# Decayed causal attention in front of a mixer MLP: two key blocks per query block, guarded by a test on the chip, and attention spread over the whole program

## The chip, the cores and the metric

The kernel runs on one core of one Trainium2 chip. The time is the device time in microseconds (us) of one execution. Every comparison below was run in rounds on one chip, with the kernel before run in the same rounds. The ratios use fast runs only. Because the program uses one core, a run can be called slow only by being more than 1.5% above the fastest run of the same kernel.

## The reference

Eight batches, eight heads, 576 tokens, head dimension 64. Attention has a causal mask and a bias that decays with the distance in a running sum of `s`. Its output, with the heads side by side (512 channels), goes through a mixer: an MLP over the tokens (576 to 256 to 576) with a residual, then an MLP over the channels (512 to 1536 to 512) with a residual.

```python
scores = scale * np.matmul(q, k.transpose(0, 1, 3, 2))          # scale = 1/8
cum = np.cumsum(np.maximum(s, 0.0), axis=-1)
bias = -(cum[:, :, :, None] - cum[:, :, None, :])
scores = np.where(causal, -1000000000.0, scores + np.minimum(bias, 0.0))
scores = scores - np.max(scores, axis=-1, keepdims=True)
attn = np.exp(scores)
attn = attn / (np.sum(attn, axis=-1, keepdims=True) + 1e-09)
x = ...np.matmul(attn, v), heads side by side: (8, 576, 512)
h = np.maximum(x.transpose(0, 2, 1) @ w_tok1, 0.0) @ w_tok2
u = x + h.transpose(0, 2, 1)
out = u + np.maximum(u @ w_ch1, 0.0) @ w_ch2
# inputs: s is drawn as randn * 0.5; q, k and v as randn * 0.1
```

The bias of key j seen from query i is `cum[j] - cum[i]`. The part `-cum[i]` is the same for all keys of a row and cancels in the softmax, so the kernel works with unnormalised weights `exp(score) * exp(cum[j] - cum[end]/2)`: the second factor is multiplied into v once.

## The kernel before

Work is recorded as operations in a plan: each has the tiles that it reads and writes, the engines that may do it with an assumed cost, and a priority. A list scheduler on the host picks, for each engine, the ready operation of lowest priority, and so fixes the order of every engine's instructions before the launch. The engines then run that order in sequence. An operation late in its engine's order waits there even if its data is ready early.

Attention goes by pairs of heads (32 pairs). Per pair, q and k are transposed, and scores are computed transposed (keys on partitions) in seven pieces that cover the causal half of 576 x 576:

```python
PIECES = [[(0, 0, 256)], [(0, 256, 512)], [(0, 512, 576), (1, 384, 576)], [(1, 128, 384)],
          [(2, 256, 512)], [(2, 512, 576), (3, 384, 576)], [(4, 512, 576)]]   # (key block, first query, last query)
...
for pc, piece in enumerate(PIECES):
    ...
        for (jc, a, e, c0) in cols:                                            # L473, PE
            nc.tensor.matmul(out=o[:, :, c0 : c0 + e - a], lhsT=kT.t[:, jc * 128 : jc * 128 + 128],
                             rhs=qT.t[:, :, a:e], start=True, stop=True)
    P.op({"PE": (occ, occ + 0.3, mm)}, ..., prio=(1, pi, 1))
    for (jc, a, e, c0) in cols:
            nc.scalar.activation(out=E.t[:, :, d0 : d0 + e - a], in_=i[:, :, c0 : c0 + e - a],
                                 func=AF.Exp, scale=0.125)                     # L481, ACT
            ...
            nc.vector.tensor_tensor(out=E.t[:, :, d0 : d0 + n], ...            # L489, DVE: causal mask of the
                in1=keep[:, 0:n]..., op=ALU.mult)                              # diagonal block, both inputs in SBUF
...
for ic in range(NJ):                                                           # L510, PE: 15 per head
    for jc in range(ic + 1):
        nc.tensor.matmul(out=o[:, ic, 0 : D + 1], lhsT=E.t[:, hh, d0 : d0 + 128],
                         rhs=vp.t[:, jc, h + hh, 0 : D + 1], start=(jc == 0), stop=(jc == ic))
```

The priorities decide how attention and the MLP are mixed. In the kernel before, the token MLP of batch `unit` has `(0, unit, ...)`, the attention pair `pi` has `(1, pi, ...)` and the channel MLP has `(2, unit, ...)`. So a pair always goes ahead of channel work, and channel work fills what is left; attention is over at about 235 us and the rest is MLP alone.

Weights arrive as fp32, are staged in the buffers that later hold the hidden layer of the channel MLP, and are cast to bf16 on whichever engine the plan chose. PE is TensorE, ACT is ScalarE, DVE is VectorE, POOL is GpSimd. "c1" and "c2" below are the first and second channel layer.

The softmax here doesn't subtract the row's maximum and nothing guards it: scores larger than these inputs give would overflow.

## Time and profile before

| | value |
|---|---|
| time | 373.82 us median of 3 runs (373.78 to 378.82) |
| span of the profiled run | 373.2 us |
| PE busy | 91% |
| start of the first c2 matmul | 84.88 us |
| end of the last add | 369.17 us, 4.0 us before the end of the span |

From the page of the kernel before, the span, the busy times of the engines, and the busy tenths of PE, DVE, ACT and DMA in 40 slices of the span:

```profile
span 373.2 us, 7668 instructions
PE 340.0 (91%) x2949; PEld 198.0 (53%) x2949; DVE 207.2 (56%) x498; ACT 228.3 (61%) x504; POOL 93.5 (25%) x129
...
PE   1875987989999989998999999999999999999994
DVE  7897577597778878667886667513302302302021
ACT  4795794877669768777878686750460660450810
DMA  9999999999996382616122010002102002102012
```

PE is nearly full from the tenth slice on (9 is 90% or more; two slices before the last show 8). DVE and ACT are well loaded up to slice 26; after that DVE is down to 0 to 3 tenths and ACT works in bursts: attention has ended. The DMA engines are full for the first 12 slices, 112 us.

A busy PE is not a PE at its limit, because matmuls overlap. The Trainium skill says so too ("Trainium Kernel Development and Optimization", Performance Expectations: matmul busy time is a bad measure because matmuls are pipelined). So I count PE **issue**: the time from start to start in back-to-back streams, 216 ns for 512 columns, 30 ns for an AV matmul, about 45 ns for a q/k transpose. The first of these can be read off the last twelve matmuls of c2 in the timeline of the kernel before (start, duration, engine, line, operation, count):

```profile
365.69 2.75 PE L688 MATMUL pmx_118<-wc_68,gb_108 128*128 128x512 bf16 x12
```

The last of the twelve takes 379 ns by itself (the mean of this group on the page), so (2.75 - 0.379) / 11 = 216 ns from start to start. Summed over the instructions, the issue is 318.5 us before: q/k transposes 17.3, scores 43.2, AV 28.8, token layers 34.6, transposes of u 8.1, channel layers 93.3 each (the terms add up to 318.6 because each is rounded). What the span has beyond that, 54.7 us, is time in which PE had nothing to start.

### The profile page before, as it was taken

How to read it: one execution, taken by the hardware profiler on the slowest of the kernel's cores; microseconds unless marked ns; L12 is line 12 of the kernel's file. 1: busy time of each engine (PE TensorE's matmuls, PEld its weight loads, DVE VectorE, ACT ScalarE, POOL GpSimd, SP SyncE). 2: the span in 40 equal slices, each digit the busy share in tenths (PEclk: the TensorE clock that was granted, in tenths of full speed). 3: DMA queues.
4: the chain of work that ended last, by engine and by line, in shares of the span. 5: the costliest groups of instructions: out<-in, count | busy, mean ns of one | idle time of the engine just before them, and what ended most of it. 6: DMA issues, size and time to landing. Idle time of an engine off the chain costs nothing.

```text
span 373.2 us, 7668 instructions
## 1 busy us (share of the span) xinstructions
PE 340.0 (91%) x2949; PEld 198.0 (53%) x2949; DVE 207.2 (56%) x498; ACT 228.3 (61%) x504; POOL 93.5 (25%) x129
## 2 busy tenths in 40 slices
PE   1875987989999989998999999999999999999994
PEld 0543535446657657564555656764444664445741
DVE  7897577597778878667886667513302302302021
ACT  4795794877669768777878686750460660450810
POOL 2427733274443552643342300000000000000000
PEclk9999898999999999999999999999999999999998
DMA  9999999999996382616122010002102002102012
GB/s 183 259 333 231 256 291 210 193 317 241 271 223 154 99 181 70 190 57 198 52 65 64 31 58 29 2 2 92 50 0 84 31 0 86 56 2 88 24 58 85
DMA packets 59173, 45.87 MB, mean 123 GB/s; under 512 B 39296, under 2 KB 52160, under 8 KB 59136
## 3 DMA queue, kind: packets, MB, share of 16 engines
q1 hardware_dynamic: 59136, 45.38, 47.7%
q8 instruction: 23, 0.38, 0.4%
q14 instruction: 14, 0.11, 0.1%
HBM read 35.93 MB, written 9.44 MB: 122 GB/s over the span
## 4 chain that ended last, share of the span: by engine, by line
PE 68%; DVE 13%; DMA 8%; ACT 7%; issue 2%; POOL 1%; SPq 0%; ACTq 0%; DVEq 0%; POOLq 0%
PE pmx_118 L688 9%; PE pmx_120 L688 8%; PE pmx_120 L669 8%; PE pmx_119 L669 7%; PE pmx_118 L669 7%; PE pmx_119 L688 6%; DMA gb_108<-in_moe_w_ch_dram 4%; PE psc_114 L473 3%; PE psc_115 L473 3%; PE psc_113 L473 3%; DMA qkf_73<-in_k_dram 3%; PE pmx_119 L603 2%; PE pav_117 L510 2%; DVE ua_101 L630 2%; PE pav_116 L510 2%
## 5 line engine op out<-in xcount | busy, mean ns | idle before, releaser
L669 PEld LDWEIGHTS <-wc_67 128*128 128x128 bf16 x576 | 55.7, 98 | 37.4 <-issue 1.9
L688 PEld LDWEIGHTS <-gb_108 128*128 128x128 bf16 x240 | 23.1, 98 | 26.3 <-issue 0.4
L688 PEld LDWEIGHTS <-ga_107 128*128 128x128 bf16 x192 | 18.3, 97 | 19.8 <-issue 0.5
L489 DVE TENSOR_TENSOR E_86<-E_86,keep 128x256 bf16<-128x256 bf16 (+1 forms) x55 | 18.6, 355 | 11.3 <-ACT E_86 L481 10.9
L385 POOL TENSOR_TENSOR vp_91<-vf_89,wT 128x512 bf16<-128x512 f32 (+1 forms) x20 | 20.6, 1058 | 14.9 <-PE pav_117 L510 13.1
L489 DVE TENSOR_TENSOR E_87<-E_87,keep 128x256 bf16<-128x256 bf16 (+1 forms) x50 | 18.9, 391 | 9.7 <-ACT E_87 L481 9.2
L489 DVE TENSOR_TENSOR E_85<-E_85,keep 128x256 bf16<-128x256 bf16 (+1 forms) x55 | 22.3, 425 | 3.6 <-ACT E_85 L481 3.3
L669 PE MATMUL pmx_119<-uTb_106,wc_67 128*128 128x320 bf16 x132 | 23.3, 299 | 0.0
L669 PE MATMUL pmx_120<-uTb_106,wc_67 128*128 128x320 bf16 x132 | 23.3, 299 | 0.0
L669 PE MATMUL pmx_118<-uTb_106,wc_67 128*128 128x320 bf16 x120 | 21.2, 299 | 0.0
L688 PE MATMUL pmx_118<-wc_68,ga_107 128*128 128x512 bf16 x84 | 20.6, 379 | 0.0
L676 ACT ACTIVATE ga_107<-pmx_120 128x512 bf16<-128x512 f32 x16 | 9.6, 601 | 17.6 <-PE pmx_120 L669 17.4
L688 PE MATMUL pmx_118<-wc_68,gb_108 128*128 128x512 bf16 x84 | 20.1, 379 | 0.0
L688 PE MATMUL pmx_120<-wc_68,gb_108 128*128 128x512 bf16 x84 | 19.9, 379 | 0.0
L676 ACT ACTIVATE gb_108<-pmx_120 128x320 bf16<-128x320 f32 x26 | 11.4, 437 | 13.9 <-PE pmx_120 L669 11.9
L676 ACT ACTIVATE gb_108<-pmx_119 128x320 bf16<-128x320 f32 x27 | 11.9, 439 | 12.9 <-PE pmx_119 L669 10.7
L669 PE MATMUL pmx_120<-uTa_105,wc_67 128*128 128x512 bf16 x76 | 19.5, 379 | 0.0
L481 ACT ACTIVATE E_85<-psc_115 128x128 bf16<-128x128 f32 (+2 forms) x37 | 15.8, 462 | 3.7 <-PE psc_115 L473 3.7
L481 ACT ACTIVATE E_86<-psc_114 128x512 bf16<-128x512 f32 (+2 forms) x36 | 15.8, 467 | 3.3 <-PE psc_114 L473 2.8
L481 ACT ACTIVATE E_85<-psc_113 128x512 bf16<-128x512 f32 (+2 forms) x31 | 15.3, 511 | 3.4 <-PE psc_113 L473 3.4
L688 PE MATMUL pmx_119<-wc_68,gb_108 128*128 128x512 bf16 x72 | 16.8, 379 | 0.0
L481 ACT ACTIVATE E_86<-psc_115 128x512 bf16<-128x512 f32 (+2 forms) x28 | 14.1, 520 | 3.9 <-PE psc_115 L473 3.9
(289 smaller groups left out, 783.2 us busy)
## 6 DMA issues: line engine op xcount, KB each, us to landing
gb_108<-in_moe_w_ch_dram SPq DMA_DIRECT2D x6, 768.0 KB, 8.8
vf_88<-in_v_dram SPq DMA_DIRECT2D x16, 256.0 KB, 5.3
vf_89<-in_v_dram SPq DMA_DIRECT2D x16, 256.0 KB, 7.9
qkf_69<-in_k_dram SPq DMA_DIRECT2D x11, 288.0 KB, 4.2
qkf_70<-in_q_dram SPq DMA_DIRECT2D x11, 288.0 KB, 4.9
qkf_71<-in_k_dram SPq DMA_DIRECT2D x11, 288.0 KB, 4.8
qkf_72<-in_q_dram SPq DMA_DIRECT2D x11, 288.0 KB, 5.2
qkf_73<-in_k_dram SPq DMA_DIRECT2D x10, 288.0 KB, 5.1
```

What stands on the lines that cost most here:

```text
L385: eng.tensor_tensor(out=vp.t[0:n, c, :, 0:D], in0=vf.t[0:n, c, :, :], in1=wT[0:n, c, b * H : b * H + H].unsqueeze(2).to_broadcast([n, H, D ...
L473: nc.tensor.matmul(out=o[:, :, c0 : c0 + e - a], lhsT=kT.t[:, jc * 128 : jc * 128 + 128], rhs=qT.t[:, :, a:e], start=True, stop=True)
L481: nc.scalar.activation(out=E.t[:, :, d0 : d0 + e - a], in_=i[:, :, c0 : c0 + e - a], func=AF.Exp, scale=0.125)
L489: nc.vector.tensor_tensor(out=E.t[:, :, d0 : d0 + n], in0=E.t[:, :, d0 : d0 + n], in1=keep[:, 0:n].unsqueeze(1).to_broadcast([128, 2, n]), ...
L510: nc.tensor.matmul(out=o[:, ic, 0 : D + 1], lhsT=E.t[:, hh, d0 : d0 + 128], rhs=vp.t[:, jc, h + hh, 0 : D + 1], start=(jc == 0), stop=(jc ...
L603: nc.tensor.matmul(out=pm.t[:, :], lhsT=w1[odd][:, c, t * 128 : t * 128 + 128], rhs=x.t[:, c, :], start=(c == 0), stop=(c == NJ - 1))
L630: nc.vector.tensor_tensor(out=dst.t[lo:hi, di, :], in0=pm.t[lo:hi, :], in1=x.t[lo:hi, c, :], op=ALU.add)
L669: nc.tensor.matmul(out=pm.t[:, 0 : e - a], lhsT=wc1[:, m, cc * 128 : cc * 128 + 128], rhs=uT.t[:, m, a:e], start=(m == 0), stop=(m == NMC ...
L676: lambda cc=cc, pm=pm, a=a, e=e: nc.scalar.activation(out=g.t[:, cc, a:e], in_=pm.t[:, 0 : e - a], func=AF.Relu),
L688: nc.tensor.matmul(out=pm.t[:, :], lhsT=g.t[:, cc, c * 128 : c * 128 + 128], rhs=wc2[:, cc, :], start=(cc == 0), stop=(cc == NCC - 1))
```

## The change

The decay makes far keys vanish. So each 128-query block looks only at its own key block and the one before it. That is safe only if the decay is strong enough over the skipped keys and no score is large, so a test on the chip checks it: a scan of the decay weights, the total decay, and the sums of squares of q and k, each over twelve rows of 64. If any entry fails, a branch at the end recomputes everything for all keys with a slow, plain routine (its body is left out below).

```diff
-    PIECES = [[(0, 0, 256)], [(0, 256, 512)], [(0, 512, 576), (1, 384, 576)], [(1, 128, 384)],
-              [(2, 256, 512)], [(2, 512, 576), (3, 384, 576)], [(4, 512, 576)]]
+    PIECES = [[(0, 0, 256)], [(1, 128, 384)], [(2, 256, 512)], [(3, 384, 576), (4, 512, 576)]]
...
-            for (jc, a, e, c0) in cols:
-                def ex(...):                       # one Exp per entry of the piece: nine per pair
+            def ex(ps=ps, pc=pc):                  # one Exp per piece: four per pair
+                nc.scalar.activation(out=E.t[:, :, EB[pc] : EB[pc] + 256],
+                                     in_=ps.t[:, :].rearrange("p (e n) -> p e n", e=2), func=AF.Exp, scale=0.125)
...
-                    for jc in range(ic + 1):
+                    j_lo = max(ic - 1, 0)
+                    for jc in range(j_lo, ic + 1):  # AV: nine per head instead of fifteen
...
+            P.op(act(768, lambda n=n, col=col: nc.scalar.activation(      # 64 of these on ACT
+                out=junk[:, :], in_=n.t[:, :, :, :].rearrange("p r e d -> p (r e d)"), func=AF.Square,
+                accum_out=sq[:, col : col + 1])), reads=[(n, 0)], writes=[("sq", col)], prio=3)
...
+    P.op(dve(64, lambda: nc.vector.tensor_scalar(
+        out=bad[0:PR, 4:], in0=sq[:, :], scalar1=10.5, scalar2=None, op0=ALU.is_gt)), ...)
+    # bad is summed over partitions by a matmul with ones, then on DVE into one int32 flag
+    need = nc.values_load(flagi[0:1, 0:1], min_val=0, max_val=4096)
+    with tc.If(need > 0, preferred_fallthrough_block=False):
+        general(ctx, tc, q, k, v, out, cum, ident, w1, w2, wc1, wc2)
...
-   pair: prio=(1, pi, i)      tok: prio=(0, unit, i)        c1: prio=(2, unit, 0)                c2: prio=(2, unit, 1)
+   pair: prio=(np_, i)        tok: prio=(rank - TOK, i)     c1: prio=(rank + 2.0 * cc / NCC, 0)  c2: prio=(rank + 2.0 + 2.0 * c / NJ, 1)
+   np_ = (b * H + h) / 2      rank = 4 * (b + 1) + LAG, LAG = TOK = 2.0
```

The last lines gather the changes of priority in one place. There are 4 pairs per batch, so `np_` and `rank` count in the same unit: the channel work of a batch is now spread over four pairs, beginning two pairs after its own last one. The change also stores the last 64 rows of odd batches differently (one copy of `w1` instead of two, no pads in `E`), which I treat as part of the window.

On these inputs the recomputation isn't taken: worked out on the host, the worst decay is 0.49 of its limit, the largest sum of squares 9.13 against 10.5, the largest total decay 132 against 160. So no run here takes the branch, and whether the recomputation is right isn't shown by them.

## The prediction

> **What bounds the kernel now.** The page gives PE 91% busy and 68% of the chain of waits. But busy overlaps in a pipelined PE, so I use start-to-start times from the timeline: 216 ns for a 512-column matmul, 30 ns for a 65-column AV matmul with its weight load (15 in 0.45 us), about 45 ns per q/k transpose. Over the instruction counts that is 318 us of PE issue: MLP 229, scores 43, AV 29, transposes 17. The other 55 us of 373 are stalls:
> - 0 to 85 us: the first second-channel-layer matmul (it needs all weights) starts at 84.9 us, with only 48 us of issue done: 37 us of stall. The DMA share is 0.94 to 1.28 in every 10 us up to 110, near 250 GB/s; the last of wc2 comes after 19.7 MB, its cast runs at 78.9 us. The chain holds DMA pieces of 6.2, 7.3, 9.5 and 6.4 us here.
> - 85 to 368 us: 270 us of issue, 13 us of stall.
> - Tail: 4.8 us after the last matmul.
>
> v packets are 256 B (39,296 packets under 512 B). The Trainium skill, "DMA: Bandwidth & Descriptors", names at least 512 B for line rate; the trace agrees in direction (stretches rich in v move 200 to 220 GB/s, others 280 to 310).
>
> **Removed.** Per head pair, score columns fall from 3200 to 2048 (0.48 us), AV matmuls from 30 to 18 (0.36 us): 15.5 + 11.5 = 27 us of PE issue over 32 pairs, leaving 291. On ACT nine Exp become four (busy 4 x 0.60 + 2 x 0.51 + 3 x 0.29 becomes 4 x 0.60): 60 us less.
>
> **Added.** 64 Square passes over 96x768 on ACT; a cast of that shape takes 0.83 us, so 53 us: ACT ends roughly where it was. One 1.35 us scan, small compares, one tiny matmul, a flag read on all engines and a branch. I evaluated the test on these inputs: worst decay ratio 0.49 of its limit, sum of squares 9.13 against 10.5, cumulative sum 132 against 160. The recomputation is never taken.
>
> **Moved.** Priorities now rank MLP chunks beside pairs, so attention is spread through the program instead of ending near 235 us; the built order shows it.
>
> **On the critical path.** The DMA order hardly changes: again 19.7 MB before the last wc2. Work cut from the first 80 us only lengthens the wait there. In the new order 41.5 us of issue precede the first second-channel-layer matmul (48 before); I expect it at 80 us. After it, 250 us of issue (270 before): of the 27 us saved only these 20 count in full. Stalls after it: 9 us, as ACT and DVE load is spread. Tail 4.8, plus 2 for flag read and branch.
> 80 + 250 + 9 + 4.8 + 2 = **346 us**, 8 in 10 within 336 to 357. Faster by over 2%: 0.95; within 2%: 0.04; slower: 0.01.
>
> **What would show it.** Windows: first second-channel-layer matmul at 77 to 84 us with DMA share near 1 until then; PE above 97% busy afterwards. Groups: 160 score matmuls, 576 AV, Square near 53 us. Attention until about 330 us; PE's last matmul 6 to 8 us before the end.
>
> **What would make it wrong.** (a) Weights arrive earlier because q/k buffers turn round sooner: 335. (b) Squares hold the four cast buffers and sit in ACT's in-order queue, so they may delay transposes, loads and Exp: 355 or more. (c) A costly branch or flag read at the end.

## More of the kernel before

Busy time by stretches of the kernel before (start:end, length, then PE, PEld, DVE, ACT and POOL busy with their counts, PE clock, DMA share, GB/s):

```profile
core 0: us, PE busy (x) PEld busy (x) DVE busy (x) ACT busy (x) POOL busy (x), PEclk, DMA share, GB/s
0.00:85.00 85.00, 63.22 (x610) 36.88 (x611) 65.46 (x163) 62.27 (x131) 39.61 (x61) 0.96 1.10 252
85.00:200.00 115.00, 110.51 (x1215) 69.40 (x1214) 88.72 (x222) 88.01 (x207) 50.67 (x64) 1.00 0.59 149
200.00:340.00 140.00, 137.79 (x964) 75.85 (x963) 48.20 (x108) 68.37 (x147) 3.19 (x4) 1.00 0.10 37
```

Up to 85 us PE is busy for 63 us, and only 48 us of issue are done. From 85 to 200 us PE is 96% busy and DVE 77%. From 200 us on PE is 98% busy and the others have much room.

## The result, and the profile after

The changed kernel takes 354.61 us (median of 4 runs, 351.32 to 356.49), beside 374.17 us for the kernel before (4 runs, 373.78 to 378.82). The ratio is 0.9441, 95% interval 0.9338 to 0.9544: faster by 5.6%. Ratios here are the mean time of one kernel's fast runs over that of the other's in the same rounds, so not quite the ratio of the quoted medians. The output is correct.

The same lines of the page, of the changed kernel:

```profile
span 352.3 us, 6579 instructions
PE 313.6 (89%) x2440; PEld 178.9 (51%) x2440; DVE 216.1 (61%) x510; ACT 225.4 (64%) x451; POOL 102.3 (29%) x131
...
PE   1674879977999999998899999988999999999990
DVE  7995587875277774777546955784657755440020
ACT  4987578974288774867787656868687647226400
DMA  9999999999732892259224421344000020011031
```

PE falls from 91% to 89% busy although the kernel is faster. DVE and ACT are loaded until slice 36: attention is spread over the whole program.

The stretches of the changed kernel:

```profile
0.00:85.00 85.00, 59.47 (x486) 33.54 (x487) 67.07 (x165) 61.86 (x116) 48.28 (x63) 0.89 1.09 258
85.00:200.00 115.00, 112.69 (x919) 66.58 (x917) 73.62 (x167) 81.31 (x169) 37.23 (x47) 1.00 0.50 129
200.00:340.00 140.00, 137.69 (x1021) 77.32 (x1022) 73.98 (x177) 82.20 (x166) 16.85 (x21) 1.00 0.19 59
```

From 200 to 340 us DVE now does 74 us of work where it did 48, and PE is as full as before. From 85 to 200 us DVE does 74 where it did 89.

The first c2 matmul and the last add, from the timeline, before and after (start, duration, engine, line, operation):

```profile
84.88 1.02 PE L688 MATMUL pmx_118<-wc_68,ga_107 128*128 128x512 bf16 x4
...
368.48 0.69 DVE L699 TENSOR_TENSOR of_112<-pmx_118,ub_102 128x512 f32<-128x512 f32 x1 [1.90 <-PE pmx_118 L688]
```

```profile
85.80 2.90 PE L817 MATMUL pmx_122<-wc_70,ga_109 128*128 128x512 bf16 x12
...
343.74 0.69 DVE L828 TENSOR_TENSOR of_114<-pmx_120,us_106 128x512 f32<-128x512 f32 x1 [1.90 <-PE pmx_120 L817]
```

These split the span into three stretches, in us; issue is the counted PE issue in them:

| stretch | before | issue | idle | after | issue | idle | change of idle |
|---|---|---|---|---|---|---|---|
| to the first c2 | 84.9 | 48.0 | 36.9 | 85.8 | 41.5 | 44.3 | +7.4 |
| to the end of the last add | 284.3 | 270.5 | 13.8 | 258.6 | 250.0 | 8.6 | -5.2 |
| after it | 4.0 | 0 | 4.0 | 7.9 | 0 | 7.9 | +3.9 |
| sum | 373.2 | 318.5 | 54.7 | 352.3 | 291.5 | 60.8 | +6.1 |

The change takes 27.0 us of issue off PE and adds 6.1 us of idle PE: that is the 20.9 us between the two profiled spans. Three questions follow. Why did the 6.5 us of work taken from the start gain nothing there? What does the test cost? And is the gain in the middle the window's, or the new order's?

### The profile page after: what moved, and what is told of

Its sections match the earlier page's. It is cut to its first block, busy times and chain, and to the rows that moved or that the text cites. A ratio compares the mean times of both kernels' runs of the same rounds, so it can differ in the third digit from the quotient of the medians.

```text
span 352.3 us, 6579 instructions
## 1 busy us (share of the span) xinstructions
PE 313.6 (89%) x2440; PEld 178.9 (51%) x2440; DVE 216.1 (61%) x510; ACT 225.4 (64%) x451; POOL 102.3 (29%) x131
## 4 chain that ended last, share of the span: by engine, by line
PE 65%; DVE 16%; ACT 11%; issue 2%; DMA 2%; POOL 1%; ACTq 0%; POOLq 0%
PE pmx_122 L817 8%; PE pmx_120 L799 8%; PE pmx_121 L799 8%; PE pmx_120 L817 8%; PE pmx_122 L799 8%; PE pmx_121 L817 6%; ACT junk L560 5%; DVE E_87 L629 3%; DVE ub_104 L760 2%; PE pav_118 L647 2%; PE psc_117 L615 2%; PE psc_115 L615 2%; PE pav_119 L647 2%; PE psc_116 L615 2%; PE pmx_121 L737 2%
## 5 line engine op out<-in xcount | busy, mean ns | idle before, releaser
L799 PEld LDWEIGHTS <-wc_69 128*128 128x128 bf16 x576 | 54.8, 99 | 34.8 <-issue 0.2
L521 POOL TENSOR_TENSOR vp_93<-vf_91,wT 128x512 bf16<-128x512 f32 (+1 forms) x20 | 20.6, 1045 | 15.7 <-PE pav_119 L647 12.4
L629 DVE TENSOR_TENSOR E_88<-E_88,keep 128x256 bf16<-128x256 bf16 (+1 forms) x55 | 18.7, 365 | 9.7 <-ACT E_88 L621 9.6
L629 DVE TENSOR_TENSOR E_87<-E_87,keep 128x256 bf16<-128x256 bf16 (+1 forms) x55 | 19.7, 388 | 7.4 <-ACT E_87 L621 7.2
L799 PE MATMUL pmx_120<-uTb_108,wc_69 128*128 128x320 bf16 x132 | 23.9, 304 | 0.0
L799 PE MATMUL pmx_121<-uTb_108,wc_69 128*128 128x320 bf16 x128 | 23.2, 304 | 0.0
L799 PE MATMUL pmx_122<-uTb_108,wc_69 128*128 128x320 bf16 x124 | 21.9, 299 | 0.0
L629 DVE TENSOR_TENSOR E_89<-E_89,keep 128x256 bf16<-128x256 bf16 (+1 forms) x50 | 15.6, 337 | 9.6 <-ACT E_89 L621 9.4
L817 PE MATMUL pmx_120<-wc_70,gb_110 128*128 128x512 bf16 x84 | 19.6, 379 | 0.0
L817 PE MATMUL pmx_122<-wc_70,gb_110 128*128 128x512 bf16 x84 | 19.6, 379 | 0.0
L521 POOL TENSOR_TENSOR vp_92<-vf_90,wT 128x512 bf16<-128x512 f32 (+1 forms) x15 | 15.4, 1045 | 9.6 <-PE pav_119 L647 9.5
L817 PE MATMUL pmx_122<-wc_70,ga_109 128*128 128x512 bf16 x72 | 17.3, 381 | 0.0
L817 PE MATMUL pmx_120<-wc_70,ga_109 128*128 128x512 bf16 x72 | 16.8, 379 | 0.2 <-ACT uTb_108 L780 0.2
L817 PE MATMUL pmx_121<-wc_70,gb_110 128*128 128x512 bf16 x72 | 16.8, 379 | 0.0
L799 PE MATMUL pmx_120<-uTa_107,wc_69 128*128 128x512 bf16 x64 | 16.6, 381 | 0.0
L799 PE MATMUL pmx_121<-uTa_107,wc_69 128*128 128x512 bf16 x64 | 16.4, 379 | 0.0
L799 PE MATMUL pmx_122<-uTa_107,wc_69 128*128 128x512 bf16 x64 | 16.4, 379 | 0.0
L549 POOL CAST qkn_79<-qkf_75 96x768 bf16<-96x768 f32 x5 | 4.1, 823 | 39.2 <-ACT ga_109 L806 19.4
```

Of the source, the lines that this page charges most:

```text
L521: eng.tensor_tensor(out=vp.t[p0 : p0 + n, c, :, 0:D], in0=vf.t[p0 : p0 + n, c, :, :], in1=wT[p0 : p0 + n, cw, b * H : b * H + H].unsqueeze ...
L549: nc.gpsimd.tensor_copy(out=n.t[:, :, :, :], in_=i)
L629: nc.vector.tensor_tensor(out=E.t[:, :, d0 : d0 + n], in0=E.t[:, :, d0 : d0 + n], in1=keep[:, k0 : k0 + n].unsqueeze(1).to_broadcast([128, ...
L799: nc.tensor.matmul(out=pm.t[:, 0 : e - a], lhsT=wc1[:, m, cc * 128 : cc * 128 + 128], rhs=uT.t[:, m, a:e], start=(m == 0), stop=(m == NMC ...
L817: nc.tensor.matmul(out=pm.t[:, :], lhsT=g.t[:, cc, c * 128 : c * 128 + 128], rhs=wc2[:, cc, :], start=(cc == 0), stop=(cc == NCC - 1))
```

## The experiments

The theory that I start from is the prediction's: the window takes 27 us off PE, the start is set by the arrival of weights, the test is nearly free, and the new order is a detail worth a few us. The rivals are: the Squares or the branch cost several us (test); the start is set by casts, or by the engines that feed attention, not by bytes (start); and without the new order the window would gain little, because another engine would then set the pace (order), with ACT, which carries the Squares, and DVE, which carries the masks, as the two candidates. Each text was written before its batch ran; where one uses a letter, it stands for the theory that the sentence around it describes (C: under the old order another engine sets the pace, ScalarE with its Squares first of all; E: the first c1 is paced by the attention pairs that stand before it in PE's order, not by loaded bytes; F, its rival: it starts when its weights are there). The batches ran on four chips; each compares with its own runs of the kernel before.

An overview of the profiled runs, all fast; spans and places in us. "Idle" is the span less the counted PE issue (318.5 for the kernel before and the one with only new priorities, else 291.5):

| kernel | median | ratio of fast runs, 95% | span | first c1 | first c2 | last add to end | idle |
|---|---|---|---|---|---|---|---|
| before | 374.17 | 1 | 373.2 | 49.8 | 84.9 | 4.0 | 54.7 |
| after | 354.61 | 0.944 (0.934 to 0.954) | 352.3 | 55.1 | 85.8 | 7.9 | 60.8 |
| x1_nosq | 350.46 | none (2 of 4 runs slow) | 347.4 | 53.3 | 82.3 | 8.4 | 55.9 |
| x2_notest | 343.50 | 0.917 (0.913 to 0.921) | 342.3 | 54.6 | 82.1 | 4.0 | 50.8 |
| x3_nobranch | 353.08 | 0.941 (0.936 to 0.946) | 345.6 | 56.0 | 83.1 | 4.2 | 54.1 |
| x4_wc2act | 353.05 | 0.943 (0.938 to 0.948) | 351.0 | 56.5 | 84.5 | 8.0 | 59.5 |
| x5_nowc2 | 351.87 | 0.939 (0.935 to 0.944) | 350.1 | 57.6 | 84.1 | 7.6 | 58.6 |
| x11_nov | 354.37 | 0.945 (0.940 to 0.950) | 351.5 | 54.8 | 84.7 | 8.5 | 60.0 |
| x14_loads | 371.16 | 0.989 (0.984 to 0.995) | 369.5 | 57.2 | 97.2 | 7.9 | 78.0 |
| x15_weights | 356.04 | 0.948 (0.944 to 0.953) | 356.9 | 53.8 | 74.1 | 7.8 | 65.4 |
| x7_b_newprio | 366.22 | 0.973 (0.968 to 0.979) | 364.0 | 51.8 | 80.1 | 2.9 | 45.5 |
| x6_oldprio | 369.79 | 0.986 (0.980 to 0.993) | 366.9 | 52.7 | 80.0 | 8.6 | 75.4 |
| x13_old_nosq | 364.04 | 0.973 (0.967 to 0.978) | 362.1 | 51.9 | 78.5 | 8.4 | 70.6 |
| x16_old_nomask | 351.31 | 0.936 (0.929 to 0.942) | 349.7 | 48.9 | 77.9 | 8.2 | 58.2 |

### What the test costs

**x1_nosq: no Square passes.** The Square operations stay in the plan, so the order of all other instructions is unchanged, but nothing is issued for them; the branch stays. The result is correct here.

```diff
-            P.op(act(768, lambda n=n, col=col: nc.scalar.activation(... func=AF.Square, accum_out=...)),
+            P.op(act(768, lambda: None),
                  reads=[(n, 0)], writes=[("sq", col)], prio=3)
+    nc.vector.memset(sq[:, :], 0.0)
```

> The changed kernel with the 64 Square passes not issued; the order of everything else is the same, the flag and the branch stay (the sums of squares are set to zero). Theory A (the passes cost time because they stand in ACT's in-order queue before Exp, copies and ReLU that PE waits for; they are 4.9% of the chain, 17 us): 344 to 349 us, and the first second-channel-layer matmul moves from 85.8 us to below 82 us. Rival B (ACT has room, 64% busy, so they are hidden behind PE and the loads): 352 us or more and the same first second-channel-layer matmul.

Measured: 350.46 us median, but from 346.46 to 352.47, with two of the four runs slow, so no ratio. The place where time went is clearer in the profiled run: last add ended at 339.02 us (344.43 with the Squares), first c2 at 82.31 (85.80), tail 8.4 us. So in this pair of profiles 5.4 us go with the Squares, up to the last add, and the tail stays.

**x2_notest: no Squares and no branch.** Also without the flag's reading and the `If`; it has no guard any more.

```diff
-    need = nc.values_load(flagi[0:1, 0:1], min_val=0, max_val=4096)
     fast_ctx.close()
-
-    with tc.If(need > 0, preferred_fallthrough_block=False):
-        general(ctx, tc, q, k, v, out, cum, ident, w1, w2, wc1, wc2)
```

> As the run without Square passes, and also without the flag's read, the branch and the recomputation's code. Theory A: the tail from the end of the last matmul to the end of the span falls from 8.6 us to about 4.8 us as in the kernel before, so 3 to 4 us less than the run without Square passes. Rival B (the tail is longer because the last rows go out as two transfers of 64 rows): the tail stays at about 8 us.

Measured: 343.50 us (342.93 to 344.12), ratio 0.9168. The last add of the profiled run in the timeline, beside the span of 342.3 us:

```profile
span 342.3 us, 6423 instructions
...
337.61 0.69 DVE L827 TENSOR_TENSOR of<-pmx,us 128x512 f32<-128x512 f32 x1 [1.90 <-PE pmx L816]
```

The add ends at 338.30, 4.0 us before the end, just as before the change. The last rows still go out as two transfers, so these aren't what lengthens the tail. Against the changed kernel, the profiled runs differ by 10.0 us: 3.7 up to the first c2, 2.4 from there to the last add, 3.9 after it. By the ratios it is 0.9441 - 0.9168 = 0.0273 of the kernel before, 10 us.

**x3_nobranch: Squares and flag computed, no branch.** The same deletion, on the changed kernel.

> The changed kernel with the Square passes, the comparison and the flag still computed, but the flag not read and no branch or recomputation code. Theory A (the branch costs time only after the last row is added): 350 to 351 us, 4 us less than the changed kernel; the time from the end of the last add to the end of the span is 4.0 us as in the kernel before instead of 7.9; the rest of the trace is unchanged (first second-channel-layer matmul at 84 to 86 us). Rival B (reading the flag also holds engines during the run): more than 5 us less, with a shorter middle.

Measured: 353.08 us, from 347.75 to 354.61, two of four slow; ratio 0.9410, which rests on the three runs of the rounds, without the profiled one, so on two that are slow beside it. The profiled run has the tail of 4.2 us after the last add. But its first c2 is at 83.10 us, though up to there it is the changed kernel, which had 85.80; and the medians of x1 and x3 together give back only 5.7 of the 11.1 us of x2. With only the runs called fast (means of 347.8 us for x1 and 349.8 us for x3, beside 354.3 for the changed kernel and 343.5 for x2) they give back 6.4 and 4.5 us, together the 10.8 us of x2. But two fast runs each are few, and two of the four runs called slow had a higher granted clock (0.978 and 0.979) than every fast one (0.964 to 0.975), so this looks like scatter. So the total of Squares and branch (10 us) and the tail (every kernel with the branch has 7.6 to 8.6 us after the last add, every one without it 2.9 to 4.2) stand; the share of the Squares before c2 is uncertain by the run-to-run scatter, 2.7 us between x3 and the changed kernel. The scan, the compares and the flag's sum stay in all three, so their cost isn't measured; nor is the flag's reading parted from the branch.

The Squares themselves, in the trace of the changed kernel (duration in ns as lowest, median, highest; first and last start in us):

```profile
L560 ACT ACTIVATE junk<-qkn_77 x16: 830/842/850, 5.7 to 265.8; 96x768 bf16<-96x768 bf16 x16
L560 ACT ACTIVATION_READ_ACCUMULATOR junk<-qkn_77 x16: 186/188/208, 6.5 to 266.6; 96x1 f32 x16
```

A Square is two instructions, 842 ns for the pass and 188 ns to read the accumulated sum, which the prediction left out. Their busy time, overlaps counted once, is 60 us. The chain of waits, which had no such group before, shows them on the path (only the line with the groups, of the changed kernel):

```profile
PE pmx_122 L817 8%; PE pmx_120 L799 8%; PE pmx_121 L799 8%; PE pmx_120 L817 8%; PE pmx_122 L799 8%; PE pmx_121 L817 6%; ACT junk L560 5%; DVE E_87 L629 3%; DVE ub_104 L760 2%; PE pav_118 L647 2%; PE psc_117 L615 2%; PE psc_115 L615 2%; PE p
```

"ACT junk L560 5%" is some 18 us of chain, more than taking the Squares out gives back. The chain tells what was waited for, not what would be won.

### What sets the start

In the trace of the changed kernel, two casts of c2 weights on POOL and two mask multiplies on DVE end together. DVE first, then POOL:

```profile
73.31 0.29 DVE L629 TENSOR_TENSOR E_89<-E_89,keep 128x256 bf16<-128x256 bf16 x1 [2.30 <-ACT E_89 L621]
74.12 1.23 DVE L629 TENSOR_TENSOR E_89<-E_89,keep 128x256 bf16<-128x256 bf16 x1
77.61 1.54 DVE L629 TENSOR_TENSOR E_87<-E_87,keep 128x256 bf16<-128x256 bf16 x1
...
73.74 1.47 POOL L677 CAST wc_70<-gb_110 128x1536 bf16<-128x1536 f32 x1
77.47 1.54 POOL L677 CAST wc_70<-gb_110 128x1536 bf16<-128x1536 f32 x1 [2.26 <-DMA gb_110<-in_moe_w_ch_dram]
```

A mask takes 0.29 us undisturbed, and 1.23 and 1.54 us while a cast runs; they end within 0.15 us of the casts. This agrees with the Trainium skill ("SBUF — State Buffer", Who interferes with whom): a DVE instruction with two SBUF inputs contends with a GpSimd instruction that reads SBUF, and the pair of ports that they share is an exclusive lock.

**x4_wc2act: those casts on ACT.** The plan, and so the order, is unchanged, apart from the engine that issues the casts of c2's weights.

```diff
-                if e == 0:
+                if e == 0 and key[0] != "wc2":
                     nc.gpsimd.tensor_copy(out=d, in_=i)
                 elif e == 1: ...
                 else:
                     nc.scalar.copy(out=d, in_=i)
```

> The changed kernel, with the two casts of the second channel weights that GpSimd does at 73.7 and 77.5 us moved to ACT, in the same place of the order. Theory A (VectorE's mask multiplies, two SBUF inputs, are blocked while GpSimd's casts hold the port they share; four masks took 1.2 to 2.0 us there instead of 0.29 us, and x of the next batch waited for them): the masks near 74 and 78 us fall below 0.7 us each, the first second-channel-layer matmul comes 1 to 3 us earlier (83 to 85 us), the time falls 1 to 3 us. Rival B (the masks are long for another reason, or do not matter): masks still over 1 us or the first second-channel-layer matmul within 0.5 us of 85.8.

Measured: the masks there are down to 0.28 to 0.29 us, from the same view:

```profile
74.61 0.29 DVE L629 TENSOR_TENSOR E<-E,keep 128x256 bf16<-128x256 bf16 x1 [2.30 <-ACT E L621]
75.42 0.28 DVE L629 TENSOR_TENSOR E<-E,keep 128x256 bf16<-128x256 bf16 x1
76.22 0.28 DVE L629 TENSOR_TENSOR E<-E,keep 128x256 bf16<-128x256 bf16 x1
```

First c2 came at 84.49 (85.80), the time is 353.05 us, ratio 0.9427 beside 0.9441. The wait of the masks is real and was removed; no gain clear of the scatter shows (x3, which has it, had its first c2 at 83.10).

**x5_nowc2: c2's weights neither loaded nor cast.** Wrong (weights are zero). It takes 3.1 MB in four staged transfers and their casts out of the start.

```diff
-               lambda st: nc.sync.dma_start(out=st[:, :]..., in_=moe_w_ch2[g * 384 : g * 384 + 384, :]...),
-               lambda st: [(wc2[:, g * 3 : g * 3 + 3, :]..., st[:, :])], ("wc2", g), 2.1)
+               lambda st: None,
+               lambda st: [], ("wc2", g), 2.1)
+    nc.gpsimd.memset(wc2[:, :, :], 0.0)
```

> Wrong result on purpose: the second channel weights are not loaded or cast (set to zero at the start); 3.1 MB less to load before the first second-channel-layer matmul, order otherwise the same. Theory P (the prediction: the start waits for the bytes of the weights at about 250 GB/s): the first second-channel-layer matmul comes about 12 us earlier, at 73 us, and the time falls by as much, to about 342 us. Rival A (the start is paced by the order in which PE takes attention and by the ACT and VectorE queues): it moves only by what the GpSimd casts cost, to 82 to 85 us, and the time stays at 350 us or more.

Measured: first c2 at 84.05 us, 351.87 us in all. Without waiting for a byte of these weights, c2 starts 1.8 us earlier. The run has a flaw: the memset of the weights holds POOL for 5.2 us at the start, and the first c1 came at 57.6 us instead of 55.1. Taking those 2.5 us off as well, c2 would be at 81.5, which is an estimate; so these weights account for some 4 us of the start at most. Even that isn't clear of the scatter: x3, which loads these weights and is the changed kernel up to there, had its first c2 at 83.10.

The traces with the weights say it directly. In the changed kernel the last cast of c2's weights (POOL, shown above) ends at 79.01 us, 6.8 us before the first c2. What PE waited for in between are a sum of the token layer and an output of attention, both from DVE:

```profile
79.93 0.38 PE L772 MATMUL pmx_120<-ident,ub_104 128*128 128x128 bf16 x4 [1.60 <-DVE us_105 L760]
...
82.72 0.66 PE L647 MATMUL pav_118<-vp_92,E_87 128*128 128x65 bf16 x9 [1.96 <-DVE x_96 L659]
```

In the kernel before, the last cast ends at 80.38 us, 4.5 us before its first c2 (84.88):

```profile
78.91 1.47 ACT L544 CAST wc_68<-gb_108 128x1536 bf16<-128x1536 f32 x1
```

The prediction's reason for the start, that c2 waits until 19.7 MB have come, doesn't hold for the changed kernel, and in the trace of the kernel before these weights weren't the last thing that c2 waited for either.

**x11_nov: v loaded for the first batch only.** Its output is wrong, which doesn't matter for the time. It takes 8.3 MB out of the transfers, and all later packets of 256 bytes.

```diff
+            if b:
+                load = lambda: None
             P.op({"SP": (0.6, 0, load)}, writes=[(vf, c)], ...)
+    # the two vf tiles are zeroed once
```

> Wrong result on purpose: v is loaded for the first batch only (the buffers are set to zero once), which takes 8.3 MB of 256-byte packets out of the loads, 2.1 MB of them ahead of the last of the first channel weights; everything on the engines stays. Theory A (until the first first-channel-layer matmul, at 55.1 us, PE waits for loaded bytes): that matmul comes at 44 to 49 us, the first second-channel-layer matmul at 68 to 77 us, and the time falls by 8 to 15 us, to 340 to 347. Rival B (that stretch is paced by the chain through PE, ACT and VectorE and by PE's lower clock there): that matmul stays at 52 us or later and the time at 350 us or more.

Measured: 354.37 us, first c1 54.8, first c2 84.7, all as with v. The stretch from 40 to 60 us, of the changed kernel and then of this one:

```profile
40.00:60.00 20.00, 16.52 (x138) 8.90 (x136) 16.28 (x41) 16.63 (x30) 12.89 (x13) 0.83 1.09 296
```

```profile
40.00:60.00 20.00, 15.94 (x134) 8.74 (x134) 16.59 (x39) 15.96 (x31) 11.25 (x11) 0.83 0.53 126
```

The DMA share falls from 1.09 to 0.53 and PE's busy time doesn't rise (16.5 and 15.9 of 20 us). So full DMA engines in this part were no sign of a wait. The Trainium skill ("DMA: Bandwidth & Descriptors", Specifications) asks for transfers of at least 512 bytes for line rate; v's packets of 256 bytes break that, and the loads go slower where v is rich (200 to 220 GB/s against 280 to 310 in the prediction's reading; no run changed the packet size alone), but taking v's loads away gained nothing here.

**x14_loads and x15_weights: weights first.** x14 also has x4's edit; it loads the weights earlier and has the planner count DMA at 1.5 times its cost. x15 is x14 with the loads of v held back in the plan.

```diff
     stage_qk(0, 0)
     stage_v(0)
-    for h in range(2, H, 2):
-        stage_qk(0, h)
-    load_tok()
-    for i in range(4): load_ch1(i)
-    stage_qk(1, 0); stage_v(1)
-    for i in range(4): load_ch2(i)
+    stage_qk(0, 2)
+    load_tok(); load_ch1(0); load_ch1(1)
+    stage_qk(0, 4); stage_qk(0, 6)
+    load_ch1(2); load_ch1(3); load_ch2(0); load_ch2(1)
+    stage_qk(1, 0); stage_v(1)
+    load_ch2(2); load_ch2(3)
...
-    dma_free = s0 + o.dma
+    dma_free = s0 + o.dma * 1.5
# x15 only:
+    loads of v of batch 1 read ("ld", ("wc1", 3)), of later batches ("ld", ("wc2", 3)), which the weight loads write
```

> The changed kernel with the weight loads asked for earlier, the scheduler told loads take 1.5 times as long as it assumed, and the two late GpSimd weight casts on ACT; in the built order 14 us of PE issue instead of 18.6 stand before the first first-channel-layer matmul, and two head pairs fewer. Theory E (the first 55 us are paced by the attention of the pairs that stand before that matmul in PE's order, each some 6 to 7 us on ACT and VectorE, not by loaded bytes): it starts 7 to 14 us earlier (41 to 48 us) and the time falls to 340 to 349 us. Rival F (it starts when its weights are there, near 50 to 55 us, whatever stands before): it stays at 50 us or later, time 350 us or more.

Measured: 371.16 us, much worse than the changed kernel. First c1 at 57.2, first c2 at 97.2: q and k of the first pairs come later, and PE waits for their casts and copies. Theory E's forecast (c1 at 41 to 48 us) failed.

> As the run with earlier weight loads, and v of the later batches is also asked for only after channel weights; 15 us of PE issue before the first first-channel-layer matmul and 30 us (41.5 in the changed kernel) before the first second-channel-layer one. Theory E: the first starts at 38 to 46 us, the second at 58 to 68 us, time 334 to 345 us. Rival F: starts at 50 us and 75 us or later, time 350 us or more.

Measured: 356.04 us, ratio 0.9484, no better than the changed kernel. First c1 moved from 55.1 to 53.8 only; first c2 came 12 us earlier, at 74.1. But the gain is given back: from 85 to 120 us PE is busy for 31.5 of 35 us, where the changed kernel had 35.0. The stretches, of the changed kernel and of x15:

```profile
85.00:120.00 35.00, 35.00 (x261) 20.84 (x260) 19.09 (x42) 23.26 (x52) 10.91 (x14) 0.98 0.51 145
```

```profile
85.00:120.00 35.00, 31.47 (x268) 19.72 (x270) 27.54 (x55) 22.42 (x51) 14.86 (x17) 0.95 0.73 155
```

An early c2 isn't a gain by itself: whichever work is brought forward, the attention that was put off has to be made up. So theory E falls in both runs: with fewer pairs ahead of it, the first c1 didn't come 7 us or more earlier. Its rival F named numbers that came near to what was measured (c1 at 50 us or later, 350 us or more; c2 at 74.1, where it said 75 or later), but its reason doesn't fit either: the last cast of c1's weights ends at 49.43 us in the changed kernel, 5.6 us before the first c1, and at 42.4 us in x15, 11.4 us before it (in x14 at 55.7 us, 1.4 us before it). For c2 it may hold in these two runs: there the last cast of its weights ends at 97.10 and 73.60 us, just before the first c2 (97.22 and 74.10). What paces the first 55 us stays open: the loads and casts of the first batch's q and k, the attention pairs on ACT and DVE, and the PE clock may all bear on it, and no run separated them. The mean clock from 30 to 60 us was 0.94 before, 0.75 in the changed kernel and 1.00 in x15, while the first c1 came at 49.8, 55.1 and 53.8 us; so the clock alone doesn't explain the later c1. A hint at DVE is x16 below: without the masks, the first c1 came 3.0 us earlier than in x13 (48.9 and 51.9).

### Window or order

**x7_b_newprio: only the new priorities, on the kernel before.** All keys, no test.

```diff
-        pi = b * H + h
+        np_ = (b * H + h) / 2
-        pair: prio=(1, pi, i)    tok: prio=(0, unit, i)      c1, c2: prio=(2, unit, 0), (2, unit, 1)
+        pair: prio=(np_, i)      tok: prio=(rank - TOK, i)   c1, c2: prio=(rank + 2.0 * cc / NCC, 0), (rank + 2.0 + 2.0 * c / NJ, 1)
```

> The kernel before with only the new priorities. Theory A: 368 to 375 us, within 2% of before. Rival B (ranking pays by itself): under 366 us.

Measured: 366.22 us beside 376.30 for the kernel before in these rounds, ratio 0.9734. With not one instruction fewer on PE, the order alone gives 2.7%. From 85 to 200 us PE is at 98.5%, where the kernel before has 96%, and DVE's load falls from 88.7 to 66.0 us:

```profile
85.00:200.00 115.00, 113.32 (x1026) 69.27 (x1035) 66.00 (x164) 67.95 (x158) 31.79 (x40) 1.00 0.49 122
```

**x6_oldprio: the window and the test, with the old priorities.** The reverse edit on the changed kernel.

> The changed kernel with the priorities of the kernel before in the scheduler (attention first, channel layers as filler). Theory A (PE already had filler, 13 us of stall after 85 us before and 8 us after, so ranking brings 0 to 5 us): 354 to 360 us. Rival B (spreading attention is what makes the change pay): over 362 us.

Measured: 369.79 us, ratio 0.9864 (0.9795 to 0.9934), which the 2% rule calls unclear. With 27 us less on PE than the kernel before, it gains 1.4%; under the new order (0.9734 to 0.9441) the same window and test gain 2.9%. So the gains of order and window don't just add up, but the difference, some 1.6%, is only just outside the combined intervals of the three ratios (an estimate: 1.4%). The idle time of PE rises to 75 us. The stretches of x6:

```profile
85.00:200.00 115.00, 100.56 (x979) 60.55 (x990) 102.35 (x243) 101.21 (x213) 55.09 (x69) 1.00 0.59 148
200.00:340.00 140.00, 137.69 (x844) 75.19 (x854) 41.54 (x85) 59.08 (x120) 0.00 (x0) 1.00 0.12 42
```

From 85 to 200 us, where all attention is packed, PE is busy for 100.6 of 115 us (87%), and DVE (102.4) and ACT (101.2) more than PE. From 200 us on PE is at 98% and DVE at 30%. The window makes PE's part of a pair cheap, so in the packed stretch another engine sets the pace; and in the pure MLP stretch the saving can't help at all. Two engines are candidates for the pace.

**x13_old_nosq: x6 without the Squares.** x1's edit on x6. It unloads ACT only.

> The changed kernel with the old priorities (369.8 us) and, in the same order, without the Square passes. Theory C (with the old priorities attention is packed into 85 to 200 us, where ACT and VectorE are both about 90% busy and PE only 78 to 90%, so there ACT and VectorE set the pace and the Square passes cost nearly their own time; with the new priorities the same passes are spread over slack): the passes cost 10 to 18 us here (352 to 360 us), against about 5 us with the new priorities. Rival D (the old order loses for a reason that has nothing to do with ACT's load): 3 to 6 us as with the new priorities, 364 us or more.

Measured: 364.04 us, ratio 0.9726. ACT is down to 63% and PE is still only at 89% from 85 to 200 us; DVE is at 93%:

```profile
85.00:200.00 115.00, 102.43 (x998) 62.72 (x1008) 107.37 (x253) 73.01 (x139) 54.17 (x68) 0.99 0.59 147
```

So ACT with its Squares isn't what holds PE here, and theory C falls in the form that names ACT: without the Squares the kernel gains 5 us, about what it gains with the new order too.

**x16_old_nomask: x13 without the mask multiplies.** Wrong (future keys count). It unloads DVE.

```diff
-                P.op(dve(2 * n, mk, True), reads=[(E, jc)], writes=[(E, jc)], prio=0)
+                P.op(dve(2 * n, lambda: None, True), reads=[(E, jc)], writes=[(E, jc)], prio=0)
```

> Wrong result on purpose: the changed kernel with the old priorities and without the Square passes (364.0 us), in the same order, and without the causal mask multiplies on VectorE (160 of them, some 54 us of its busy time). Theory G (packed attention between 85 and 200 us is paced by VectorE, 92 to 94% busy there while ACT without the Square passes is at 63%; that is why the old order wastes PE's saving): VectorE falls below 80% in that stretch, PE rises above 95%, and the time falls to 344 to 354 us. Rival H (PE's own order and the dependent steps of a pair set the pace, VectorE is busy only because it waits for GpSimd's port): PE stays under 92% there and the time stays at 358 us or more.

Measured: 351.31 us, ratio 0.9357, 3.7% of the kernel before less than x13 (0.9726). PE goes to 98%, DVE to 65%:

```profile
85.00:200.00 115.00, 112.88 (x1072) 68.26 (x1084) 74.56 (x158) 76.19 (x144) 53.72 (x68) 0.99 0.62 155
```

With the old order and an unloaded DVE, the kernel is 12.7 us faster by the medians; idle PE falls from 70.6 to 58.2 us, the level of the changed kernel. This shows VectorE's part of attention as what sets the pace when attention is packed. It doesn't part DVE's load from the delay of the mask itself in the chain from Exp to AV: the edit takes both away. And part of that load is waiting: the 103 masks of x13 in this stretch take 44.3 us, 0.43 us each, where the median mask takes 0.28 us (the longest 3.4), so some 15 us (an estimate) may be waits for POOL like those at 74 and 78 us above; x16 takes them away too. No run takes the masks away with the Squares in place.

### Versions that could beat the changed kernel

With the guard kept, x4 has the lowest time with an interval (353.05 us), but its interval and the changed kernel's overlap. x2 (343.50 us) is clearly faster, and drops the guard. A cheaper norm test than a pass of ACT over all of q and k would be the next thing to write.

## Why the prediction was right or wrong

The prediction was 346 us, within 336 to 357; measured were 354.61 us. The direction was right and the time lies inside the range, near its upper end. Point by point, the sum 80 + 250 + 9 + 4.8 + 2 against the profiled run (to the last matmul's end, where the last add starts: 343.74 us):

| term | predicted | measured |
|---|---|---|
| first c2 | 80 | 85.8 |
| from there to the last matmul's end | 250 issue + 9 stall = 259 | 257.9 |
| tail with flag and branch | 4.8 + 2 = 6.8 | 8.6 |
| sum | 346 | 352.3 (span) |

- **Only the PE saving after the start counts in full: right.** Of 27 us of issue, the 6.5 us before the first c2 gave nothing there.
- **"I expect it at 80 us", because the last of the weights comes after 19.7 MB: wrong, in the time and in the cause.** It came at 85.8 us. The last of those weights was cast 6.8 us before the first c2 (4.5 us in the kernel before), and PE then waited for DVE's part of attention and of the token layer. With those weights not loaded at all (x5) c2 came at 84.1 (81.5 by the estimate above), with 8.3 MB of v gone (x11) at 84.7. The DMA share near 1 was read as a wait; x11 halves it from 40 to 60 us and the time stays. The tests were made on the changed kernel; I did not repeat them on the kernel before.
- **Squares: undersized.** Predicted 53 us of ACT, from a cast of that shape; measured 60, because each pass has a second instruction of 188 ns. The prediction put them in the sum at nothing and named "they may delay transposes, loads and Exp" as its risk (b): taking out Squares and branch gives 10 us, of which 6 lie before the end of the last add. The other half of its sum for ACT was off too: the Exps fall from 112.2 to 67.9 us (overlaps counted once), 44 us less and not 60; ACT as a whole ends where it was (228.3 and 225.4), as it said.
- **Branch: undersized.** Predicted 2 us, measured 3.9 us.
- **"Stalls after it: 9 us, as ACT and DVE load is spread": right in size and cause, but its weight was not seen.** Measured 7.9 us. The prediction treats the spreading as 4 us saved. x6 shows that without it the window and the test gain 1.4% instead of 5.6%: 4.2% of the kernel before, about 16 us, hang on the order. And x7 shows that the order alone, with no window, gains 2.7%, so most of these 16 us would have come without the window.
- **"PE above 97% busy afterwards": right** (98% from 85 to 200 and from 200 to 340 us; the kernel before had 96% and 98%).

(The time of an execution is some 2 us above its span: the profiled run of the changed kernel took 354.19 us.) The prediction came near because its misses (start and tail, together 7.6 us late, against 1.1 us early in between) were small enough for its range, not because its account of the start was right: that the start was only 5.8 us off was luck.

## What to carry to other kernels

When a change makes the work of the busiest engine cheaper in one phase only, ask which engine is next in that phase: time is the sum over phases of the busiest engine's time, and a saving counts only where that engine had the longest share. Spreading the phase over the whole program gained here with the saving and without it, and it can be tried alone on the old kernel first. Don't take full DMA engines for a wait: leave a transfer out and look whether anything starts earlier.

## What the Trainium skill lacked or had wrong

- "Runtime: NRT & Kernel Launch", Instruction fetch mechanics, says that branching breaks the sequential prefetch and that runtime control flow is expensive, without a figure for a whole flag read and branch, which the skill's timings of single branch instructions don't cover. Here a flag read on the engines and an untaken recomputation at the end cost 3.9 us: 7.9 us from the last add to the end with it, 4.0 without.
- "ScalarE: Activation LUTs", What it computes, mentions the accumulator output but not that reading it is an instruction of its own. Here each `accum_out` added an instruction of 188 ns to a pass of 842 ns, 64 times.
- "TensorE: Matmul & The Clock Gate", Back-to-back issue gap, gives about 131 ns per matmul of 512 columns as the sustained rate of a stream of weight loads and matmuls. No stream that I read reaches that: the twelve matmuls of c2 shown above, each with its own weights, start 216 ns apart. The same section's isolated gap, about 216 ns, is what this trace shows.
- "TensorE: Matmul & The Clock Gate", Part 1, tells of the clock falling when PE idles, and shows it on a kernel with little matmul work between its waits. It draws no warning from it that taking work off PE can cost clock: from 30 to 60 us the kernel before ran at a mean clock of 0.94, and so did x7 with all keys in the new order; the changed one, with less attention work on PE, ran at 0.75, and x1 to x5 and x11, which share its window and order, at 0.74 to 0.78. Whether that cost time is not settled: another load order (x15) ran that stretch at 1.00 and reached the first c1 only 1.3 us earlier.
